# Squared-ReLU attention and two MLPs: the short last row of each batch read from mirror blocks, loads two tiles a time, MLP steps at row ends

## The chip, the core and the metric

The program runs on one core of a Trainium2 chip. TensorE (PE) multiplies, with a separate record for the loading of weights (PEld); VectorE (DVE) and ScalarE (ACT) work elementwise; GpSimd (POOL) and SyncE (SP) mostly issue DMAs here. The metric is the device time of one execution in microseconds, as the median of several.

## What is computed

```python
B, S, D = 2, 3008, 256          # d_qk = 64, d_ff = 2048
scores = z @ z.T / S            # per batch, symmetric
x = u * (relu(scores)**2 @ v)   # 6016 x 256 over both batches
h = x @ w_in                    # first MLP, w_in and w_out given as float64 ("moe")
P = a[0] + a[1]*h + a[2]*h**2 + a[3]*h**3
Q = 1 + abs(b[0])*abs(h) + abs(b[1])*h**2
x = (P / (Q + 1e-6)) @ w_out
h = x @ w_in2                   # second MLP ("moe2")
out = (max(h, 0) + alpha*min(h, 0)) @ w_out2
```

## The kernel before

All products are made from fp32 values split into a high and a low part, so one product takes several matmuls: high by high, high by low, low by high.

**Attention.** A batch has six query blocks j, here called rows: five of 512 queries and a last one of 448 (`qn`). Keys go in pairs of 128-key tiles, 12 pairs kp in a batch, and a *step* is one row with one pair: 12 steps a row, 144 in both batches. A key block kb = kp // 2 has the 512 keys (or last 448) of the query block with that number. A *direct* step in `a_scores` makes four score matmuls (two tiles, two matmuls each with zA and zB), then ScalarE takes ReLU and scale out of PSUM (L836, L844) and squares (L849), and `hi_lo` splits the result r into ahi (ScalarE, L438) and alo (VectorE, L443). Since scores are symmetric, a block above the diagonal is the transpose of one below. Where `folded(b, j, kb)` holds, the direct step is followed by `turn_block`: VectorE transposes r in 32 x 32 pieces into rt (L760), and four DMAs write it to DRAM (L771). When row kb later comes to that pair, its step is *folded*: no score matmuls, one load of rr from DRAM (L804), then `hi_lo`. Before, `folded` asks for a full 512-query row, so the last row of a batch is direct in all 12 steps. `in_turns` mixes folded and direct steps of a row evenly. Rows of 512 queries hold their columns in a permuted order (`q_side`, and `swap` on the host) that the piecewise transposes bring about; the last row does not.

Three steps later (`LAG_A`), `a_values` multiplies r with v: 8 matmuls for ahi (L870) and 4 for alo (L881), into one accumulator. At the end of a row, `a_end` loads u and multiplies on VectorE (L914), which frees the accumulator for the next row, and writes the product to DRAM for the MLP.

`load_z` and `load_v` load and split z and v: all of a batch's tiles are put into the program at the start of its first row. v is split by a cast (ScalarE, for the most part) and a subtraction (VectorE, L443) into vt.

**MLPs.** 6016 tokens go in 12 blocks, each with 8 steps in either MLP. A step has 12 matmuls into h or m (L941 to L943) and 12 back (L870, L881). A first-MLP step has seven VectorE operations on 128 x 1024 (L1000 to L1012) and six on ScalarE; a second-MLP step two and three. Weights are decoded from float64 (`weight`), those of the first MLP stay in SBUF, those of the second go to DRAM and come back in 16 fills (`fill_w`, L641) through GpSimd's queue, all put in at the end of attention.

**Order.** The program is put down in one order for TensorE; for the other engines and SP's queue a planner (`Plan.order`) sorts by due times, worked backward from TensorE's order. While the attention steps are put down, `plan.debt` adds VectorE's planned time and subtracts `FILL` times TensorE's; whenever it is below `DEBT` (plus `EDGE` where a row has just ended, which is seen at the third step of the next row), the next item of a list `extra` is put in: a weight or a first-MLP step (from step `HEAD` on). `X1` first-MLP steps are in the list; the rest runs in the tail with the second MLP, after attention. SBUF work tiles share 48 equal rooms.

Of the kernel before, what the change touches and what calls it, by code (L numbers as in the profile page):

```python
# [28 lines left out]

WIRE = 0.6  # L30

FILL, DEBT, EDGE = 0.95, 4.0, 4.0

LAG_A, LAG_M = 3, 2

HEAD, X1 = 40, 21

R0, RD = 2, 2.5

# [259 lines left out]
def relu2_attention_rational_mlp_prelu_mlp(  # L299
# [13 lines left out]
    nc = tc.nc  # L313
    P = 128
# [5 lines left out]
    NJ = NF // 2  # L320
    QB = 512
    NQ = -(-S // QB)
    NK = -(-S // P)
    NKP = NK // 2
# [4 lines left out]
    qn = [min(QB, S - j * QB) for j in range(NQ)]  # L329
# [10 lines left out]
    plan = Plan({"p": PT, "z": ZP, "x": XP, "s": 2, "h": 1, "acc0": 1, "acc1": 1, "m": 1, "sr": 1})  # L340
# [12 lines left out]
    def room(nm, dtype=F32, shape=(P, 2, QB)):  # L353
        return Buf("p", lambda i: pt.tile(list(shape), dtype, tag=f"p{i}", name=nm))

    def big_room(nm):
        return room(nm, F32R, (P, 2, 2, 256))
# [10 lines left out]
    def h_room(nm):  # L368
        return Buf("h", lambda i: at["h"][i])
# [15 lines left out]
    def in_dram(shape, nm, parts=1, dtype=F32):  # L385
        t = dr.tile(shape, dtype, name=nm)
        return Buf(None, lambda _: t, parts)
# [7 lines left out]
    def pe(cols, count, fn, r, w):  # L395
        return plan.add("PE", count * (cols / 2400 + 0.0136), fn, r, w)

    def sp(kb, fn, r, w, level="load", rate=210.0, horizon=NEAR):
        return plan.add("SP", 0.5, fn, r, w, level, after=3.0, data=kb / rate, horizon=horizon)

    def pool_dma(kb, fn, r, w, level="dec", rate=180.0, horizon=FAR):
        return plan.add("POOL", 1.1, fn, r, w, level, after=3.0, data=kb / rate, horizon=horizon)
# [233 lines left out]
    def fill_w(store, jp, in_room):  # L636
        d = store[jp]
        t = room("w", F32R, (P, 2, 2, 256)) if in_room else big_room("w")
        pool_dma(
            512,  # L640
            lambda: nc.gpsimd.dma_start(out=t().rearrange("p k c d -> p k (c d)"), in_=d()),  # L641
            [d],
            [t],
            level="load",
            rate=250.0,
        )
        store[jp] = t

    zA = {}

    zB = {}

    def q_side(z, b, j):

        if qn[j] < QB:
            return z[b, j]()[:, : qn[j]]
        return z[b, j]().rearrange("p (s a r) -> p a s r", s=4, a=4)

    def load_z(b, g):

# [71 lines left out]
        zB[b, j] = t  # L732

    def folded(b, i, j):
        return i < j and qn[j] == QB

    def in_turns(b, j):
        first = [kp for kp in range(NKP) if folded(b, kp // 2, j)]
# [7 lines left out]
    order = {q: in_turns(*q) for q in blocks}  # L746

    direct = [0]
    turned = {}

    def turn_block(b, j, kp, r):

        kb, h = kp // 2, kp % 2
        if (b, j, kb) not in turned:
            turned[b, j, kb] = in_dram([4, P, QB], f"rt{b}_{j}_{kb}", 8)
        d = turned[b, j, kb]
        t = room("rt", F32, (P, 4, 4, 2, 32))
        dve(
            1024,
            lambda: nc.vector.transpose(  # L760
                t().rearrange("p s a i x -> p i a s x"), r().rearrange("p i (g x) -> p i g x", x=32)
            ),
            [r],
            [t],
            level="turn",
        )
        for a in range(4):
            x0 = a * P + h * 64
            sp(
                128,  # L770
                lambda a=a, x0=x0: nc.sync.dma_start(  # L771
                    out=d()[:, :, x0 : x0 + 64].rearrange("s (a r) x -> r (s a) x", r=32),
                    in_=t()[32 * a : 32 * a + 32].rearrange("r s a i x -> r (s a) (i x)"),
                ),
                [t],
                [(d, 4 * h + a)],
                rate=150.0,
            )
# [18 lines left out]
    def a_scores(b, j, kp):  # L797
        n = qn[j]
        if folded(b, kp // 2, j):
            r, d = room("rr"), turned[b, kp // 2, j]  # L800
            s0 = kp % 2 * 2
            sp(
                512,
                lambda: nc.sync.dma_start(out=r(), in_=d()[s0 : s0 + 2].rearrange("s p k -> p s k")),  # L804
                [d],
                [r],
            )
            ahl[b, j, kp] = hi_lo(r, n, kp)
            return
        r = room("r")  # L810

        pair = None
        if not opened:
            turn = kp % 3 if (b, j) == (0, 0) else direct[0] % 2
            direct[0] += 1
            if turn == 1:
                pair = h_room("sp")
            elif turn == 2:
                t2 = Buf("acc1", lambda i: at["acc1"][i])
                pair = t2  # L820
        for i in range(2):
            k = 2 * kp + i
            zk = zA[b, k // 4]
            s = (pair, i) if pair is not None else s_room("s")
            ks = slice((k % 4) * P, (k % 4 + 1) * P)

            def mm(s=s, i=i, zk=zk, ks=ks):
                o = pair()[:, i, :n] if pair is not None else s()[:, :n]
                nc.tensor.matmul(o, zk()[:, ks], q_side(zA, b, j), start=True, stop=False)  # L829
                nc.tensor.matmul(o, zk()[:, ks], q_side(zB, b, j), start=False, stop=True)  # L830

            pe(n, 2, mm, [zk, zA[b, j], zB[b, j]], [s])
            if pair is None:
                act(
                    n,
                    lambda s=s, i=i: nc.scalar.activation(r()[:, i, :n], s()[:, :n], AF.Relu, scale=1.0 / S),  # L836
                    [s],
                    [(r, i)],
                    psum=True,
                )  # L840
        if pair is not None:
            act(
                2 * n,
                lambda: nc.scalar.activation(r()[:, :, :n], pair()[:, :, :n], AF.Relu, scale=1.0 / S),  # L844
                [pair],
                [r],
                psum=True,
            )
        act(2 * n, lambda: nc.scalar.activation(r()[:, :, :n], r()[:, :, :n], AF.Square), [r], [r])  # L849
        ahl[b, j, kp] = hi_lo(r, n, kp)  # L850
        if folded(b, j, kp // 2):
            turn_block(b, j, kp, r)
# [274 lines left out]
    edge, done = [], []  # L1127

    def a_stream():

        pend = []

        def drain(upto):
            while len(pend) > upto:
                q, kp = pend.pop(0)
                a_values(*q, kp)
                if kp == order[q][-1]:
                    a_end(*q)
                    edge.append(True)

        for g in range(NQ):
            load_z(0, g)
            if g % 2 == 0 and g < NQ:
                load_v(0, 2 * g)
                load_v(0, 2 * g + 2)
        for q in blocks:
            b, j = q
            if j == 0 and b:
                for g in range(NQ):
                    load_z(b, g)  # L1150
                for kp in range(0, NKP, 2):
                    load_v(b, kp)
            a_begin(*q)
            for kp in order[q]:
                a_scores(b, j, kp)
                pend.append((q, kp))
                drain(LAG_A)
                yield
        drain(0)
        yield  # L1160
# [23 lines left out]
    fills = list(w2)  # L1184

    extra = []
# [3 lines left out]
    for k in range(max(rest, 2 * NJ)):  # L1190
        extra += [("m",)] * ((k + 1) * rest // (2 * NJ) - k * rest // (2 * NJ))
        extra += [("w", w2.pop(0), False)]
    n1 = 0
    for st in range(NB * NKP + 1):
        edge.clear()
        next(ga)
        while extra and plan.debt < DEBT + (EDGE if edge else 0):
            if st < R0:
                break
            what = next((x for x in extra if x[0] == "w" or st >= HEAD), None)  # L1200
            if what is None:
                break
            if what[0] == "w" and st < HEAD and st - R0 < RD * (sum(x[0] == "w" for x in done)):
                break
            extra.remove(what)
            done.append(what)
            if what[0] == "w":
                weight(*what[1], what[2])
            else:
                opened.append(n1)  # L1210
                next(g1s)
                next(g1s)
                n1 += 1
                edge.clear()
    for what in extra:
        if what[0] == "w":
            weight(*what[1], what[2])
    for k, f in enumerate(fills):
        fill_w(f[1], f[2], False)

    left = (NB - 1) * NJ - KEEP
    steps = NB * NJ - n1
    for st in range(steps):
        more = (st + 1) * left // steps - st * left // steps
        next(g1s)
        if st:
            next(g2s)
        if more:
            next(g2s)
        next(g1s)  # L1230
        if more > 1:
            next(g2s)
            next(g2s)
# [54 lines left out]
```

## Time and profile before

| | |
|---|---|
| median of 3 runs | 1531.78 us (1531.62 to 1534.46) |
| the profiled execution | 1532.52 us |
| its span | 1530.3 us |
| TensorE busy | 1512.1 us, 6736 matmuls |
| VectorE busy | 1393.6 us |
| ScalarE busy | 1224.8 us |
| granted TensorE clock, mean | 0.999 |

Attention takes about the first 600 us; batch 1 starts a little after 300 us. The tail holds the MLPs up to the end. Matmul ends are modelled, so the distance from one start to the next is read rather than the duration of one. A wait is the idle time of an engine before an instruction, put down to what released it.

### The profile page before, as it was taken

What the parts mean: (1) busy time and instruction counts of PE and PEld (TensorE: products, weight loads), DVE (VectorE), ACT (ScalarE), POOL (GpSimd) and SP (SyncE); (2) the same over time, 40 slices, a digit from 0 to 9 for tenths busy, and PEclk for the clock granted to TensorE, in tenths of its full rate; (3) what the DMA queues carried; (4) which work ended last, traced back from release to release, by engine and by line L of the source; (5) the groups of instructions that cost most, each with busy time, mean ns of one, the idle gap of its engine ahead of it and who ended that gap; (6) DMA issues with size and microseconds to landing.
All of it is one profiled execution on the core that took longest, in us unless ns stands there. A gap on an engine that the chain in (4) does not pass through costs nothing.

```text
span 1530.3 us, 17886 instructions
## 1 busy us (share of the span) xinstructions
PE 1512.1 (99%) x6736; PEld 1261.2 (82%) x6736; DVE 1393.6 (91%) x1429; ACT 1224.8 (80%) x1465; POOL 73.2 (5%) x98
## 2 busy tenths in 40 slices
PE   9999999999999999999999999999999999999999
PEld 7887888867788888788888888888888888888888
DVE  8999898997999996899999999999999999999963
ACT  8888888996987988878778787777877777787754
POOL 1000010011112112000000000000000000000000
PEclk9999999999999999999999999999999999999999
DMA  6986431545765635300000000000000000000000
GB/s 188 227 229 182 123 102 68 182 105 147 204 178 169 225 125 170 130 28 28 28 28 14 28 29 14 28 14 28 29 28 28 28 14 28 28 25 28 15 1 24
DMA packets 131207, 126.14 MB, mean 82 GB/s; under 512 B 90145, under 2 KB 99889, under 8 KB 131121
## 3 DMA queue, kind: packets, MB, share of 16 engines
q1 hardware_dynamic: 121488, 90.40, 19.9%
q0 software_dynamic: 9632, 34.62, 6.9%
q8 instruction: 52, 0.85, 0.2%
q14 instruction: 35, 0.28, 0.1%
HBM read 74.72 MB, written 47.45 MB: 80 GB/s over the span
## 4 chain that ended last, share of the span: by engine, by line
PE 87%; DVE 7%; ACT 3%; issue 1%; DMA 1%; SPq 1%; DVEq 0%; ACTq 0%
PE acc L870 33%; PE acc L881 17%; PE h L943 5%; PE h L941 5%; PE h L942 5%; PE m L943 5%; PE m L941 5%; PE m L942 5%; PE s L830 1%; PE s L829 1%; DVE alo L443 1%; PE acc L860 1%; ACT r L836 1%; ACT r L849 1%; DVE vt L443 0%
## 5 line engine op out<-in xcount | busy, mean ns | idle before, releaser
L870 PE MATMUL acc<-ghi,w 128*128 128x512 f32 (+1 forms) x1472 | 360.7, 387 | 0.0
L870 PEld LDWEIGHTS acc<-ghi,w 128*128 128x128 f32 x1472 | 275.6, 188 | 54.9
L870 PE MATMUL acc<-ahi,vt 128*128 128x512 f32 (+1 forms) x1152 | 284.8, 389 | 5.8 <-DVE ut L914 4.9
L870 PEld LDWEIGHTS acc<-ahi,vt 128*128 128x128 f32 x1152 | 216.6, 188 | 51.4 <-DVE ut L914 4.8
L997 ACT ACTIVATE t<-h,sc 128x1024 f32<-128x1024 f32 (+1 forms) x96 | 114.1, 1188 | 107.5 <-PE h L943 103.9
L881 PE MATMUL acc<-glo,w 128*128 128x512 f32 (+1 forms) x736 | 195.3, 387 | 1.9 <-DVE glo L1012 1.9
L1064 ACT ACTIVATE m<-m,sc 128x512 f32<-128x512 f32 (+1 forms) x182 | 117.8, 692 | 67.9 <-PE m L943 67.7
L1000 DVE SCALAR_TENSOR_TENSOR ab<-sq,cb,ab 128x1024 f32<-128x1024 f32 (+1 forms) x96 | 121.2, 1262 | 50.5 <-ACT sq L995 49.9
L881 PEld LDWEIGHTS acc<-glo,w 128*128 128x128 f32 x736 | 137.7, 188 | 30.2 <-DVE glo L1012 2.8
L943 PE MATMUL h<-xhi,w 128*128 128x512 f32 (+1 forms) x404 | 154.6, 383 | 0.0
L942 PE MATMUL h<-xlo,w 128*128 128x512 f32 (+1 forms) x404 | 154.6, 383 | 0.0
L941 PE MATMUL h<-xhi,w 128*128 128x512 f32 (+1 forms) x404 | 154.6, 383 | 0.0
L881 PE MATMUL acc<-alo,vt 128*128 128x512 f32 (+1 forms) x552 | 147.4, 387 | 1.5 <-DVE alo L443 1.5
L943 PE MATMUL m<-xhi,w 128*128 128x512 f32 (+1 forms) x364 | 140.8, 387 | 0.0
L942 PE MATMUL m<-xlo,w 128*128 128x512 f32 (+1 forms) x364 | 140.8, 387 | 0.0
L941 PE MATMUL m<-xhi,w 128*128 128x512 f32 (+1 forms) x364 | 140.7, 387 | 0.0
L443 DVE TENSOR_TENSOR glo<-m,ghi 128x1024 fp32r<-128x1024 f32 (+1 forms) x96 | 115.1, 1199 | 11.8 <-ACT ghi L438 11.8
L1005 ACT ACTIVATE sq<-ab,one 128x1024 f32<-128x1024 f32 (+1 forms) x96 | 110.3, 1149 | 17.1 <-DVE t L1002 16.8
L881 PEld LDWEIGHTS acc<-alo,vt 128*128 128x128 f32 x552 | 103.9, 189 | 22.8 <-DVE alo L443 2.7
L1009 DVE TENSOR_TENSOR ghi<-t,sq 128x1024 fp32r<-128x1024 f32 (+1 forms) x96 | 115.5, 1203 | 7.8 <-ACT sq L1006 6.8
L836 ACT ACTIVATE r<-s 128x512 f32<-128x512 f32 (+1 forms) x170 | 94.8, 601 | 32.0 <-PE s L830 31.4
L443 DVE TENSOR_TENSOR alo<-r,ahi 128x1024 fp32r<-128x1024 f32 (+1 forms) x92 | 108.9, 1188 | 11.9 <-ACT ahi L438 11.6
(99 smaller groups left out, 2726.3 us busy)
## 6 DMA issues: line engine op xcount, KB each, us to landing
rt<-rt SPq DMA_DIRECT2D x160, 128.0 KB, 3.5
rr<-rt SPq DMA_DIRECT2D x40, 512.0 KB, 4.9
wraw<-in_moe_w_in_dram POOLq DMA_DIRECT2D x16, 512.0 KB, 5.2
wraw<-in_moe_w_out_dram POOLq DMA_DIRECT2D x16, 512.0 KB, 4.9
wd<-dec POOLq DMA_DIRECT2D x16, 512.0 KB, 3.1
w<-wd POOLq DMA_DIRECT2D x16, 512.0 KB, 9.9
x2d<-x SPq DMA_DIRECT2D x11, 512.0 KB, 2.6
xr<-x2d SPq DMA_DIRECT2D x11, 512.0 KB, 3.2
```

The source lines that it names most:

```text
L443: lambda: nc.vector.tensor_tensor(lo(), src(), hi().bitcast(F32), ALU.subtract),
L836: lambda s=s, i=i: nc.scalar.activation(r()[:, i, :n], s()[:, :n], AF.Relu, scale=1.0 / S),
L870: nc.tensor.matmul(acc()[:, e, :n], w()[:, k, i, e * P : (e + 1) * P], hi()[:, i, :n], start=first and i == 0 and k == 0, stop=False,)
L881: nc.tensor.matmul(acc()[:, e, :n], w()[:, 0, i, e * P : (e + 1) * P], lo()[:, i, :n], start=False, stop=last and i == both - 1,)
L941: nc.tensor.matmul(acc, w_hi, hi, start=first, stop=False)
L942: nc.tensor.matmul(acc, w_hi, lo, start=False, stop=False)
L943: nc.tensor.matmul(acc, w_lo, hi, start=False, stop=last)
L997: act(N, lambda: activation(c(t), c(h), AF.Identity, scale=a3, bias=a2), [h], [t], psum=True, ptr=2, **kw)
L1000: dve(N, lambda: stt(c(ab), c(sq), b1, c(ab), ALU.mult, ALU.add), [sq, ab], [ab], ptr=1, **kw)
L1005: act(N, lambda: activation(c(sq), c(ab), AF.Abs_reciprocal_sqrt, bias=one), [ab], [sq], ptr=1, **kw)
L1009: dve(N, lambda: tt(c(hi), c(t), c(sq), ALU.mult), [t, sq], [hi], **kw)
L1064: lambda i=i, f=f: nc.scalar.activation(t()[:, i, :n], h()[:, i, :n], AF.Copy, scale=al[:, f : f + 1]),
```

## The change

The last row's blocks are folded too. In rows 0 to 4, the direct steps of pairs 10 and 11 are now turned and written (448 or fewer columns, in pieces of 64 or 32 columns of fp32), and 10 of the last row's 12 steps load rr of 448 columns. For that the last row's columns are permuted as well, in two parts of 256 and 192, so its two direct steps take eight matmuls of those widths instead of four of 448.

The first six loads are put down ahead of batch 0, the rest one at each step of its first row; those of batch 1 two at every second step of batch 0's last row. At the end of a row a first-MLP step that is ready goes before a weight. `HEAD` goes from 40 to 38, `X1` from 21 to 18, `FILL` from 0.95 to 0.97. The fills of the second MLP's weights are put in as six at the end of attention and two for each second-MLP step.

```diff
-FILL, DEBT, EDGE = 0.95, 4.0, 4.0
+FIRST, NEXT = 6, 4
+FILL, DEBT, EDGE = 0.97, 4.0, 4.0
...
-HEAD, X1 = 40, 21
+HEAD, X1 = 38, 18
...
-        if qn[j] < QB:
-            return z[b, j]()[:, : qn[j]]
-        return z[b, j]().rearrange("p (s a r) -> p a s r", s=4, a=4)
+        t = z[b, j]().rearrange("p (s a r) -> p a s r", s=4, a=4)
+        if qn[j] == QB:
+            return [(0, QB, t)]
+        return [(0, QB // 2, t[:, 0:2]), (QB // 2, qn[j], t[:, 2:4, 0:3])]
...
     def folded(b, i, j):
-        return i < j and qn[j] == QB
+        return i < j
...
         if (b, j, kb) not in turned:
-            turned[b, j, kb] = in_dram([4, P, QB], f"rt{b}_{j}_{kb}", 8)
+            turned[b, j, kb] = in_dram([4, P, qn[kb]], f"rt{b}_{j}_{kb}", 8)
         d = turned[b, j, kb]
...
             x0 = a * P + h * 64
+            wide = 64
+            if qn[kb] < QB and a >= 2:
+                x0 = QB // 2 + (a - 2) * 96 + h * 64
+                wide -= 32 * h
             sp(
-                128,
-                lambda a=a, x0=x0: nc.sync.dma_start(
-                    out=d()[:, :, x0 : x0 + 64].rearrange("s (a r) x -> r (s a) x", r=32),
-                    in_=t()[32 * a : 32 * a + 32].rearrange("r s a i x -> r (s a) (i x)"),
+                2 * wide,
+                lambda a=a, x0=x0, wide=wide: nc.sync.dma_start(
+                    out=d()[:, :, x0 : x0 + wide].rearrange("s (a r) x -> r (s a) x", r=32),
+                    in_=t()[32 * a : 32 * a + 32].rearrange("r s a i x -> r (s a) (i x)")[:, :, 0:wide],
                 ),
...
             sp(
-                512,
-                lambda: nc.sync.dma_start(out=r(), in_=d()[s0 : s0 + 2].rearrange("s p k -> p s k")),
+                n,
+                lambda: nc.sync.dma_start(out=r()[:, :, :n], in_=d()[s0 : s0 + 2].rearrange("s p k -> p s k")),
                 [d],
...
                 o = pair()[:, i, :n] if pair is not None else s()[:, :n]
-                nc.tensor.matmul(o, zk()[:, ks], q_side(zA, b, j), start=True, stop=False)
-                nc.tensor.matmul(o, zk()[:, ks], q_side(zB, b, j), start=False, stop=True)
-            pe(n, 2, mm, [zk, zA[b, j], zB[b, j]], [s])
+                for (c0, c1, x), (_, _, y) in zip(q_side(zA, b, j), q_side(zB, b, j)):
+                    nc.tensor.matmul(o[:, c0:c1], zk()[:, ks], x, start=True, stop=False)
+                    nc.tensor.matmul(o[:, c0:c1], zk()[:, ks], y, start=False, stop=True)
+            pe(n, 2 if n == QB else 4, mm, [zk, zA[b, j], zB[b, j]], [s])
             if pair is None:
...
-        for g in range(NQ):
-            load_z(0, g)
-            if g % 2 == 0 and g < NQ:
-                load_v(0, 2 * g)
-                load_v(0, 2 * g + 2)
+        todo = [("z", 0, 0), ("v", 0, 0), ("z", 0, 1), ("v", 0, 2)]
+        todo += [x for g in range(2, NQ) for x in (("z", 0, g), ("v", 0, 2 * g))]
+        def load(count):
+            for _ in range(count):
+                if todo:
+                    kind, b, k = todo.pop(0)
+                    (load_z if kind == "z" else load_v)(b, k)
+        load(FIRST)
         for q in blocks:
             b, j = q
-            if j == 0 and b:
-                for g in range(NQ):
-                    load_z(b, g)
-                for kp in range(0, NKP, 2):
-                    load_v(b, kp)
+            if b and j == 0:
+                load(1)
             a_begin(*q)
-            for kp in order[q]:
+            for i, kp in enumerate(order[q]):
+                if q == (0, 0):
+                    load(1)
+                elif b == 0 and j == NQ - 1 and i == NEXT - 1:
+                    todo = [x for g in range(NQ) for x in (("z", 1, g), ("v", 1, 2 * g))]
+                if todo and q != (0, 0) and i % 2 == 1:
+                    load(2)
                 a_scores(b, j, kp)
...
     n1 = 0
+    nw = 0
     for st in range(NB * NKP + 1):
...
         next(ga)
-        while extra and plan.debt < DEBT + (EDGE if edge else 0):
-            if st < R0:
+        while extra and st >= R0 and plan.debt < DEBT + (EDGE if edge else 0):
+            ready = st >= HEAD and (n1 < min(nw // 2, NJ) or n1 >= NJ)
+            k = next((k for k, x in enumerate(extra) if (x[0] == "m" and ready) or (x[0] == "w" and not (edge and ready and ("m",) in extra))), None)
+            if k is None or (extra[k][0] == "w" and st < HEAD and st - R0 < RD * nw):
                 break
-            what = next((x for x in extra if x[0] == "w" or st >= HEAD), None)
-            if what is None:
-                break
-            if what[0] == "w" and st < HEAD and st - R0 < RD * (sum(x[0] == "w" for x in done)):
-                break
-            extra.remove(what)
-            done.append(what)
+            what = extra.pop(k)
             if what[0] == "w":
                 weight(*what[1], what[2])
+                nw += 1
             else:
...
             weight(*what[1], what[2])
-    for k, f in enumerate(fills):
-        fill_w(f[1], f[2], False)
+    fill = [lambda f=f: fill_w(f[1], f[2], False) for f in fills]
+    def top(count):
+        for _ in range(min(count, len(fill))):
+            fill.pop(0)()
+    top(6)
...
         more = (st + 1) * left // steps - st * left // steps
+        top(2 * more)
         next(g1s)
...
     swap[:whole] = swap[:whole].reshape(-1, 4, 4, 32).transpose(0, 2, 1, 3).reshape(-1)
+    ends = [whole + 128 * s + 32 * a for a in range(4) for s in range(4) if 128 * s + 32 * a < seq - whole]
+    swap[whole:] = (_np.array(ends)[:, None] + _np.arange(32)).reshape(-1)
     for name in _INS:
```

## Rows read from the trace of the kernel before

**Rows 1.** The page: busy us, share of the span, instructions of each engine.

```profile
PE 1512.1 (99%) x6736; PEld 1261.2 (82%) x6736; DVE 1393.6 (91%) x1429; ACT 1224.8 (80%) x1465; POOL 73.2 (5%) x98
```

**Rows 2.** Stretches: us, busy us (instructions) by engine, granted clock, DMA share, GB/s.

```profile
core 0: us, PE busy (x) PEld busy (x) DVE busy (x) ACT busy (x) POOL busy (x), PEclk, DMA share, GB/s
0.00:300.00 300.00, 294.84 (x1294) 244.70 (x1295) 273.56 (x340) 259.19 (x323) 20.15 (x32) 1.00 0.57 164
300.00:600.00 300.00, 292.66 (x1279) 240.25 (x1278) 275.79 (x325) 258.23 (x337) 45.59 (x52) 0.99 0.54 161
425.00:575.00 150.00, 150.00 (x662) 124.08 (x662) 147.15 (x175) 125.48 (x157) 26.84 (x29) 1.00 0.53 168
50.00:100.00 50.00, 50.00 (x219) 40.75 (x218) 47.47 (x68) 43.94 (x57) 3.62 (x5) 1.00 0.88 228
358.00:362.00 4.00, 4.00 (x11) 3.15 (x12) 2.17 (x3) 4.00 (x6) 1.11 (x2) 0.57 0.59 198
900.00:1100.00 200.00, 200.00 (x884) 165.62 (x883) 191.03 (x171) 157.09 (x176) 0.00 (x0) 1.00 0.07 24
```

**Rows 3.** Waits, TensorE: us in total, times, longest.

```profile
PE acc L870 <- DVE ut L914: 4.9, 4, 1.8
PE s L829 <- ACT r L836: 2.2, 4, 0.8
PE acc L881 <- DVE glo L1012: 1.9, 2, 1.7
PE acc L881 <- DVE alo L443: 1.5, 3, 0.7
PE acc L870 <- DVE vt L443: 0.9, 1, 0.9
```

**Rows 4.** Timeline, TensorE, 300 to 360: start, us, instructions, idle time before.

```profile
316.60 1.90 PE L870 MATMUL acc<-ahi,vt 128*128 128x512 f32 x7 [0.90 <-DVE vt L443]
...
357.92 3.38 PE L870 MATMUL acc<-ahi,vt 128*128 128x512 f32 x8 [1.80 <-DVE ut L914]
```

**Rows 5.** Timeline, TensorE, one step of batch 0's last row.

```profile
257.22 0.36 PE L829 MATMUL s<-zA 128*128 128x448 f32 x1
...
258.02 1.79 PE L870 MATMUL acc<-ahi,vt 128*128 128x448 f32 x8
...
260.46 0.36 PE L829 MATMUL s<-zA 128*128 128x448 f32 x1
```

**Rows 6.** Timeline, TensorE, the last 384 tokens.

```profile
1505.54 0.33 PE L941 MATMUL m<-xhi,w 128*128 128x384 f32 x1
1505.71 0.33 PE L942 MATMUL m<-xlo,w 128*128 128x384 f32 x1
```

**Rows 7.** Groups by shape: busy us, mean ns, idle us before; score weight loads.

```profile
L829 PEld LDWEIGHTS s<-zA 128*128 128x128 f32 x170 | 32.2, 190 | 11.1 <-ACT r L836 3.9 <-DVE zA L682 1.4
```

**Rows 8.** Timeline, VectorE, 327 to 331.

```profile
327.53 2.37 DVE L760 STREAM_TRANSPOSE rt<-r 128x1024 f32<-128x1024 f32 x2
329.81 1.19 DVE L443 TENSOR_TENSOR alo<-r,ahi 128x1024 fp32r<-128x1024 f32 x1
```

**Rows 9.** Groups by shape, VectorE, 0 to 610.

```profile
L760 DVE STREAM_TRANSPOSE rt<-r 128x1024 f32<-128x1024 f32 x40 | 49.0, 1236 | 4.1 <-DMA rt<-rt 4.1
...
L1000 DVE SCALAR_TENSOR_TENSOR ab<-sq,cb,ab 128x1024 f32<-128x1024 f32 x21 | 27.0, 1287 | 13.4 <-ACT sq L995 13.3
...
L1011 DVE TENSOR_TENSOR t<-t,ab 128x1024 f32<-128x1024 f32 x21 | 25.6, 1221 | 0.1
```

**Rows 10.** DMA issues: instructions, KB of one, median us to landing.

```profile
rt<-rt SPq DMA_DIRECT2D x160, 128.0 KB, 3.5
rr<-rt SPq DMA_DIRECT2D x40, 512.0 KB, 4.9
...
w<-wd POOLq DMA_DIRECT2D x16, 512.0 KB, 9.9
...
zB<-zA SPq DMA_DIRECT2D x18, 128.0 KB, 3.9
```

**Rows 11.** Waits of VectorE and ScalarE on transfers of blocks.

```profile
DVE rt L760 <- DMA rt<-rt: 4.1, 2, 2.5
...
ACT ahi L438 <- DMA rr<-rt: 3.2, 2, 2.1
```

## The prediction

> **What bounds the kernel now.** I read the page's busy times first, then who waits for whom on TensorE, then busy times by stretch, and last the timeline of the places that these point to. TensorE is busy for 1512.1 us of 1530.3, VectorE for 1393.6 [rows 1]. A busy TensorE need not be at its peak, so look at the spacing: in the steady MLP stretch 884 matmuls fill 200 us, 0.226 us each, and 512 columns at 2.4 GHz are 0.213 of that [rows 2]. TensorE is the bound, at its pace, and VectorE runs 95.5% beside it there. All named waits of TensorE on other engines that matter come to some 11 us [rows 3]: 4.9 at four ends of rows (the values of the next row need the accumulator that VectorE still has to multiply with u), 4.6 for score evictions, vt and alo, 1.9 for glo. One of the row ends also cost clock: after 1.80 us of idle time [rows 4] the granted clock stood at 0.57 over 358 to 362 us, the 1.2 GHz level for most of it, and 11 matmuls ran where 17.7 would have [rows 2]; 6.7 times 0.226 is 1.5 us. So two things can move the time: fewer matmuls, and fewer stalls. VectorE bounds nothing on average but has little left.
>
> **Scores no longer computed.** The last row of each batch now takes 10 of its 12 steps from mirror blocks, 20 in all. Such a step before has four 448-column score matmuls, from 257.22 to 258.02 us: 0.80 us [rows 5]. All of it is on TensorE's path, in line with the value matmuls behind it (the step takes 3.24 us, it will take 2.44). 20 x 0.80 = **16.0 us less**. ScalarE loses two evictions and a square each time, which bound nothing in that row and are worth nothing by themselves.
>
> **The remaining four direct steps** of those rows issue eight matmuls of 256 and 192 columns where four of 448 stood: the same columns, 16 more instructions. Low end: a 384-column matmul follows the next by 0.17 us [rows 6], 0.013 more than its columns at 2.4 GHz, so 16 x 0.013 = 0.2. High end: no matmul shorter than the 0.19 us of its weight load [rows 7]: 8 x 0.19 less 0.80 is 0.72 a step, 2.9 in all. The 384-column ones undercut 0.19 already, so I stay near the low end: **0.6 more**. The Trainium skill (TensorE: Matmul & The Clock Gate, LDWEIGHTS) puts a load of 128 columns at 107 ns and says that it overlaps the running matmul; an estimate by that page: only the 192-column ones (0.08 us) would be held up, 16 times some 0.015 us, and the term would be 0.4. No row here has a matmul that short at the full clock.
>
> **Work that the mirror costs.** The ten blocks a batch are now turned where they are computed, as their last two steps in rows 0 to 4: 20 transposes on VectorE, 1.19 us each in line (2.37 for two) [rows 8], 1.24 alone [rows 9], so 24 us; 80 more writes on SP's queue, each landing in 3.5 us, and 20 loads of rr, 4.9 us [rows 10]. Against that, three first-MLP steps leave the attention phase (21 to 18). Each has seven VectorE operations of 1.22 to 1.29 us, from 27.0 us for 21 to 25.6 us for 21 [rows 9], 8.7 us a step, 26 in all, and 24 x 0.226 = 5.4 us of TensorE, 16.3 in all. So VectorE's work in the attention phase stays as it was, 273.56 + 275.79 = 549 us of the first 600 [rows 2], now about 547, while TensorE's part shrinks: 600 less 15.4 (the two terms above) less 16.3 less the stalls below (9) is 559 us. That is a share of 97.9% instead of 91.6%. This is the weak point of the forecast. Look at 425 to 575 us: VectorE is busy 147.15 of 150 us, 98.1%, and TensorE has no idle time [rows 2]. Such a share can be carried for 150 us by this order of work. Low end 0; high end, if the phase gets only halfway from 91.6 to 98.1%, 547 / 0.949 = 576, 17 us late. I take **3 more**, since the 150 us row is the nearest to what the whole phase will look like.
>
> The three steps that moved make the tail richer in VectorE work: 78 first-MLP steps for the same number of second ones (two VectorE operations each, so 2.4 us against 5.4 on TensorE). Scaling the 95.5% of [rows 2] by that mix gives 96.6%. Under the 98.1% just shown, so 0. The tail's TensorE work is only moved, not added.
>
> **Queues.** SP gets 100 more issues in 560 us at about half a microsecond each; they sit behind each other, not behind compute. The rr loads of a row queue ahead of the next batch's z and v on SP; ScalarE's cast of rr and through it the row's values are what waits if one is late. Over 40 loads that was 3.2 us of ScalarE [rows 11], none of it seen on TensorE; 20 more at that rate would be 1.6. I take **0.5**, from 0 to 1.6. The DMA engines were busy for 88% of 50 to 100 us and TensorE was not idle there [rows 2].
>
> **Loads two tiles a time.** Batch 1's z and v are issued through the last row of batch 0 instead of all being due at the start of batch 1. Before, their splits meet that batch's first row; TensorE waits there for vt (0.90 us at 316.60 [rows 4]) and four times for evictions that queue behind vt casts on ScalarE, 2.2 us [rows 3]. With alo's share this is about 3.5 us; 3.0 of it goes, as the last row now has few evictions of its own. What is late next there is the row end itself. The head of the kernel waits for the first z all the same: 0.
>
> **MLP steps at row ends.** The first one is now allowed from step 38, which is where the end of row 2 falls, and at an end an MLP step goes before a weight. 5.4 us of matmuls cover the 1.8 us of the longest such wait. Of 4.9 us and the 1.5 of lost clock I take 4.5 back. But the cover of one end gets thinner: between the last values of row 4 and the first of row 5 a direct score step (0.80 us) stood, and now none does, as the fourth step of that row is a mirrored one. Should no MLP step land there, both batches pay 1.8 + 1.5, so 0 to 6.6; I take **1.0**, since the rule asks for one.
>
> **Weight fills.** 16 fills of w were issued together at the end of attention and landed in 9.9 us [rows 10]; now six, then two per second-MLP step. VectorE's wait-free start of the tail should give back 1.5 of the 1.9 us that TensorE waited for glo [rows 3]. The cover for the later fills is three MLP steps of over 10 us; without it, one landing, 9.9 us. Stalls given back: 3.0 + 4.5 + 1.5 = **9.0 less**.
>
> **Sum.** 1530.3 - 16.0 + 0.6 + 3.0 + 0.5 + 1.0 - 9.0 = 1510.4 us of span. The profiled execution took 1532.5, 2.2 more than its span, and is 0.7 above the median of the runs, 1531.8. So 1510.4 + 2.2 - 0.7 = **1512 us**, 1.3% faster. A measurement of this kernel can tell about 0.2%, 3.1 us, from no change.
>
> **Rivals.** First, only the matmuls go and the stalls stay, moved to other places, because every stall is VectorE or ScalarE being late and both of these get denser: 1512 + 9 = 1521. For it: VectorE's share rises. Against it: ScalarE, which released 2.2 us of them, gets less to do. Chance 0.22.
>
> Second, slower than before: VectorE becomes the bound of the attention phase. Place: steps 0 to 144. If no batch can sustain more than the 91.6% that it shows now, the 547 us take 597 instead of 559, 38 us where I took 3, and the time is 1547: the phase is as long as it was and the tail has 16.3 us more. It decides at 93.7%: then the phase takes 600 - 16.3 us and nothing is gained. For it: neither of the two 300 us rows is above 92%. Against it: in both, the idle time of VectorE sits at the head and around the batch border, and 425 to 575 us is at 98.1% [rows 2]. Chance 0.07.
>
> Third, the transfers bind in rows 0 and 1, where eight of the 20 added blocks are written. VectorE has waited twice for a transpose buffer still being written, 4.1 us in all [rows 11]; were each of the eight to cost 2.05, it is 16 us, and with the fuller VectorE nothing would make up for it: 1528. Against it: 88% DMA share passed without harm. Chance 0.05. A rule speaks for it: the Trainium skill (DMA: Bandwidth & Descriptors, Specifications) wants at least 512 B a piece, below which a read-modify-write sets in; these writes are in pieces of 256 and 128 B. In the trace a 128 KB rt write of such pieces lands in 3.5 us and the 128 KB zB copy in 3.9 [rows 10], so the penalty does not show at the landing time.
>
> Last, the code might mirror fewer steps than it says (0.01, no change), or the stalls vanish altogether and VectorE costs nothing, under 1504 (0.05).
>
> **How the numbers follow.** Forecast, 1504 to 1517: 0.60. Faster by over 0.2%: forecast 0.60, better 0.05, first rival 0.22, and 0.03 of the third: 0.90. Within 0.2%: 0.02 of the third, 0.02 of the second, 0.01: 0.05. Slower: 0.05 of the second. Range: down to 1504 (terms of 3.0, 1.0, 0.5 and 0.4 at their low ends and the last 3 us of stalls gone), up to 1524, which takes in the first rival and most of VectorE's high end; the rest is left out.
>
> **What would show it.** 60 rr loads, 60 transposes, 84 x 4 score matmuls' worth of columns; a folded step of the last row taking 2.44 us; VectorE near 98% over the attention phase with TensorE idle under 5 us there; no wait for ut over 1 us after row 2; none for vt at the batch border. Wrong would be: attention's VectorE share under 94% with TensorE waiting for alo or glo all over (second rival), waits for rr or rt buffers in rows 0, 1 and 5 (third), or waits of the old size at the ends of rows and the border (first).

## The result

The changed kernel takes 1513.5 us (median; 1511.4 to 1514.6) against 1532.6 of the kernel before, run beside it: a ratio of 0.9872, 95% interval 0.9855 to 0.9889. 1512 was forecast. The total was right. How it comes about was not: the next sections show that the two halves of the sum, 16 us from matmuls and 9 us from stalls, cannot be had one without the other.

The busy times on the page of the changed kernel, as in [rows 1]:

```profile
PE 1497.1 (99%) x6672; PEld 1248.8 (83%) x6672; DVE 1410.0 (93%) x1449; ACT 1193.2 (79%) x1406; POOL 79.2 (5%) x98
```

Its stretches, with the columns of [rows 2]: attention up to the last values matmul at 569.4 us, the start of the tail, and the steady MLP stretch.

```profile
0.00:569.40 569.40, 560.93 (x2473) 464.01 (x2474) 541.46 (x658) 469.30 (x585) 72.27 (x86) 1.00 0.72 203
569.40:620.00 50.60, 46.89 (x194) 37.87 (x193) 46.17 (x46) 37.81 (x43) 5.88 (x12) 0.93 0.44 145
900.00:1100.00 200.00, 200.00 (x884) 165.64 (x883) 192.05 (x173) 158.69 (x176) 0.00 (x0) 1.00 0.06 22
```

Attention and the start of the tail in the kernel before, where the last values matmul ends at 607.7 us:

```profile
0.00:607.70 607.70, 595.20 (x2609) 491.93 (x2610) 553.90 (x671) 521.12 (x665) 70.53 (x93) 1.00 0.55 162
607.70:660.00 52.30, 50.37 (x221) 40.99 (x220) 42.01 (x38) 40.37 (x45) 2.67 (x5) 1.00 0.39 139
```

Attention became 38.3 us shorter (607.7 to 569.4), the tail 20.8 longer (1530.3 - 607.7 = 922.6 to 1512.8 - 569.4 = 943.4): 17.5 us off the span. By its own terms the prediction had 34.7 off attention and 14.8 more in the tail. So attention did 3.6 better than its terms and the tail 6.0 worse, and the two partly cancel. Most of the tail's 6.0 lies at its start: 194 matmuls in 50.6 us at a mean clock of 0.93, where before 221 ran in 52.3 at the full one. At 0.226 us each, 6.7 us are lost there against 2.3 before. The steady tail is untouched: 884 matmuls in 200 us, with VectorE at 96.0% (96.6 was forecast).

TensorE's waits in the changed kernel, as in [rows 3], those of its first 15 us left out:

```profile
PE acc L878 <- DVE ahi L796: 3.3, 2, 2.1
PE acc L889 <- DVE glo L1020: 3.2, 1, 3.2
PE m L949 <- DVE m L1078: 0.5, 1, 0.5
PE acc L878 <- ACT ahi L792: 0.4, 1, 0.4
PE acc L878 <- DVE ut L922: 0.4, 1, 0.4
```

And the two largest in TensorE's timeline of the same kernel:

```profile
548.88 1.86 PE L878 MATMUL acc<-ahi,vt 128*128 128x448 f32 x4 [2.13 <-DVE ahi L796]
...
596.99 2.08 PE L889 MATMUL acc<-glo,w 128*128 128x512 f32 x4 [3.17 <-DVE glo L1020]
598.87 0.63 PE L949 MATMUL h<-xhi,w 128*128 128x512 f32 x1
599.29 0.63 PE L950 MATMUL h<-xlo,w 128*128 128x512 f32 x1
```

The waits for u at row ends are gone but for 0.4 us (4.9 before), and so are those at the batch border, about 3.5 us. In their place stand a wait in each batch's last row (1.2 and 2.1 us), for the half-tile correction that VectorE makes for pair 11 (L796), and a longer one for glo where the tail starts. After the 3.17 us of idle time matmuls start 0.42 us apart instead of 0.226: the lower clock level, a granted clock of 0.50 from 597 to 603 us.

### The profile page after: what moved, and what is told of

Read it like the earlier page. It is cut to its first block, busy times and chain, and to the rows that moved or that the text cites. A ratio compares the mean times of both kernels' runs of the same rounds, so it can differ in the third digit from the quotient of the medians.

```text
span 1512.8 us, 17898 instructions
## 1 busy us (share of the span) xinstructions
PE 1497.1 (99%) x6672; PEld 1248.8 (83%) x6672; DVE 1410.0 (93%) x1449; ACT 1193.2 (79%) x1406; POOL 79.2 (5%) x98
## 4 chain that ended last, share of the span: by engine, by line
PE 74%; DVE 8%; issue 2%; ACT 1%; DMA 0%; SPq 0%; DVEq 0%; ACTq 0%
PE acc L878 26%; PE acc L889 13%; PE m L949 5%; PE m L950 5%; PE m L951 5%; PE h L949 5%; PE h L950 5%; PE h L951 5%; DVE alo L445 2%; PE acc L868 1%; PE s L837 1%; PE s L838 1%; DVE t L1019 1%; DVE ab L1018 1%; DMA rt<-rt 0%
## 5 line engine op out<-in xcount | busy, mean ns | idle before, releaser
L1078 DVE TENSOR_TENSOR m<-m 128x1024 f32<-128x1024 f32 (+1 forms) x91 | 109.7, 1205 | 11.6 <-ACT m L1072 11.5
L1020 DVE TENSOR_TENSOR glo<-t,sq 128x1024 fp32r<-128x1024 f32 (+1 forms) x96 | 114.7, 1195 | 1.4
```

Source lines behind the costliest of these rows:

```text
L1020: dve(N, lambda: tt(c(lo), c(t), c(sq), ALU.mult), [t, sq], [lo], **kw)
```

## The experiments

Each kernel ran beside the kernel before; ratios are to that, so 0.9872 is what the whole change gives. "The arrangement" is everything in the change but the mirrored last row: loads, row-end rule, `HEAD`, `X1`, `FILL` and fills.

### The mirrored row alone, and the rest alone

`fold_only`, the kernel before with the hunks of `q_side`, `folded`, `turn_block`, `a_scores` and `swap`:

```diff
-        return i < j and qn[j] == QB
+        return i < j
```

> The kernel before with the mirrored last row alone: 64 fewer matmuls, but loads, the rule at row ends, the list of MLP steps (21, from step 40, fill 0.95) and the weight fills as they were. Theory (TensorE is the bound and the matmuls are the gain; the other parts give and take stalls): 1532.6 less the 15.8 us of matmuls, stalls as before or some us more, 1515 to 1522. Rival (VectorE sets the attention phase, and only the shift of three MLP steps into the tail pays for the 24 us of transposes): 1530 or more.

Measured: 1534.9 us, ratio 1.0019 (1.0009 to 1.0028). The matmuls went and the time stayed. The rival's number was right. Its stretches, attention up to 581.2 us and what follows:

```profile
0.00:581.20 581.20, 565.19 (x2473) 466.83 (x2474) 531.26 (x634) 468.04 (x579) 69.73 (x79) 0.99 0.69 194
581.20:640.00 58.80, 46.84 (x191) 36.60 (x190) 57.53 (x71) 40.32 (x48) 15.16 (x20) 0.94 0.56 188
```

And TensorE's longest waits in it:

```profile
PE acc L876 <- DVE ut L920: 8.9, 5, 2.7
PE acc L887 <- DVE glo L1018: 6.3, 2, 4.8
PE acc L887 <- DVE alo L443: 3.3, 2, 2.6
```

Look at 581 to 640 us: VectorE is busy for 57.53 of 58.80 us while TensorE is idle for 12. Work for VectorE that belongs to the attention phase has been left for the start of the tail; the last weight's decoding (its addition, L575) starts at 608.8 us there, 27.6 us after attention's end, where before it started at 598.4, ahead of the end. That is not all of it: for the same 2473 matmuls attention is 11.8 us longer than in the changed kernel (581.2 against 569.4), the rest 8.4 (951.8 against 943.4), so more than half of the 20 us between the two is lost inside attention.

`no_fold`, the changed kernel with those same hunks undone:

```diff
-        return i < j
+        return i < j and qn[j] == QB
```

> The changed kernel without the mirrored last row: loads, row ends, step list and fills are the new ones. Theory: the full number of matmuls, the waits for u at row ends and at the batch border gone (some 10 us of lost time before), a new wait of some 6 us where the tail starts: 1526 to 1530. Rival (the gain is mostly the freed stalls): 1518 or less.

Measured: 1530.7 us, ratio 0.9985 (0.9976 to 0.9994). The arrangement alone gives 0.15%, some 2 us, just above the range expected here and far from the 9 us of the prediction. Its waits on TensorE (a part of them): those for u are gone but for 0.6 us, and others have come.

```profile
PE acc L883 <- DVE glo L1014: 2.8, 1, 2.8
PE s L831 <- ACT r L838: 2.1, 3, 0.9
PE h L945 <- DVE w L445: 1.5, 1, 1.5
PE acc L872 <- DVE ut L916: 0.6, 1, 0.6
```

So one half costs 0.2%, the other gives 0.15%, and both together give 1.28%. On the new arrangement the mirrored row is worth 0.9985 - 0.9872 = 1.1%, 17 us, the 16 of its matmuls and a little; on the old one it is worth less than nothing. I read this as the arrangement making room for the 24 us of transposes; the next runs test it.

### How much room VectorE has

`turn_twice`, the changed kernel with each of the 20 added blocks transposed twice:

```diff
+        def turn():
+            for _ in range(2 if qn[kb] < QB else 1):
+                nc.vector.transpose(...)
```

> The changed kernel with each of the 20 added blocks transposed twice on VectorE, everything else in the same order: 20 x 1.19 = 24 us more VectorE work in the attention phase, which there is at 541 us of 569. Theory (VectorE has little left, 95% busy): some of it shows, 4 to 15 us. Rival 1 (VectorE is already the bound of the phase): 20 us or more. Rival 2 (it has slack that the transposes fill): under 3 us.

Measured: 1533.5 us, ratio 1.0008 (0.9998 to 1.0017), 1.36% or 21 us above the changed kernel. The number is that of rival 1. Its attention phase, ending at 590.5 us:

```profile
0.00:590.50 590.50, 569.35 (x2473) 465.52 (x2474) 566.55 (x680) 471.56 (x586) 70.81 (x88) 0.99 0.70 196
```

The same 2473 matmuls, 25.1 us more of VectorE (541.46 to 566.55), and the phase is 21.1 us longer, 0.84 us for each. But the cost is not spread evenly. Both kernels issue the same matmuls in the same order, so stretches between the same matmuls can be laid side by side. Four of the changed kernel:

```profile
135.00:235.00 100.00, 100.00 (x444) 82.50 (x443) 96.35 (x104) 82.67 (x97) 2.89 (x4) 1.00 0.56 156
235.00:262.00 27.00, 25.80 (x127) 22.92 (x126) 26.81 (x31) 21.23 (x26) 0.00 (x0) 1.00 0.74 240
460.00:500.00 40.00, 40.00 (x178) 32.95 (x176) 39.90 (x49) 32.40 (x39) 7.01 (x8) 1.00 0.81 232
500.00:550.00 50.00, 47.44 (x222) 40.55 (x221) 49.88 (x69) 37.17 (x48) 12.75 (x13) 0.98 0.78 251
```

And the same four in `turn_twice`:

```profile
135.40:236.50 101.10, 100.25 (x444) 82.39 (x443) 99.44 (x106) 79.23 (x92) 3.04 (x4) 1.00 0.53 152
236.50:270.20 33.70, 28.54 (x129) 23.99 (x129) 33.51 (x38) 25.59 (x33) 0.00 (x0) 0.96 0.73 222
474.40:514.60 40.20, 40.20 (x177) 32.62 (x175) 40.04 (x50) 30.73 (x36) 5.84 (x8) 1.00 0.79 221
514.60:571.10 56.50, 49.55 (x226) 41.62 (x226) 56.30 (x75) 41.11 (x53) 11.23 (x14) 0.97 0.73 232
```

Before the first of them, 523 matmuls take 120.0 us in both kernels, with five of the added blocks in the stretch. All ten of batch 0 start before 236.5 us and have cost about 1.5 us by then; 6.7 more come out in the next stretch, 27 us in the changed kernel, where VectorE was full already (26.81 us) and now has 38 operations to do instead of 31. In batch 1, 6.2 are lost from 345 to 460 us, where VectorE was at 96.8%, and 6.5 from 500 to 550, where it was at 99.8%. Between them, a stretch at 99.6% loses 0.2. So VectorE bounds parts of the phase, the ends of the batches above all, and lets work in for nothing elsewhere; the mean shares of 95.1 and 95.9% are no ceiling. With 8.5 us of 569 idle on TensorE, the page calls the whole phase bound by TensorE.

`x1_21`, `x1_16`: the changed kernel with 21 or 16 MLP steps in the list instead of 18.

```diff
-HEAD, X1 = 38, 18
+HEAD, X1 = 38, 21    # the other: 38, 16
```

> The whole changed kernel with 21 MLP steps in the list instead of 18: everything else, loads, row ends and fills, is the new form. Two weights are then left over at the end of attention. Theory A: slower by the VectorE time of three MLP steps less what their 16.3 us of TensorE work gives in the phase, 5 to 12 us, 1519 to 1526, with longer waits where the tail starts. Theory B: within 2 us of 1513.5.

> The whole changed kernel with 16 MLP steps in the list: the last weight is put in at step 138 of 144 instead of 143. Theory A: VectorE gets through before the tail, the 3.2 us wait for glo at the tail's start with its stretch at the lower clock and the waits of the last row shrink: 1508 to 1512; the tail then has 80 first-MLP steps and must not wait for VectorE. Rival: VectorE's share in the tail, 96.6% by the sum, goes to some 97.4% and shows there: 1514 or more.

Measured: with 21 steps 1523.1 us, ratio 0.9938 (0.9923 to 0.9953), 0.66% or 10 us slower than with 18. With 16 steps 1515.5 us, ratio 0.9887 (0.9873 to 0.9902), whose interval overlaps that of 18: no gain. The wait for glo at the tail's start did not shrink with 16 either (3.2 us again), although the last weight's addition (L577) starts 2.7 us behind the end of attention there and 9.6 us behind it in the changed kernel. So the late last weight is not what makes it, and my reading of that wait was wrong. The wait stands some 27 us behind the end of attention in both kernels, and the kernel before has one of 1.69 us at the like place, 25.5 us behind. Its cause stays open. Attention and the start of the tail with 21:

```profile
0.00:578.40 578.40, 570.64 (x2521) 472.35 (x2522) 549.95 (x656) 479.63 (x593) 80.20 (x82) 1.00 0.70 196
578.40:640.00 61.60, 49.05 (x195) 37.99 (x195) 57.67 (x67) 41.84 (x50) 8.43 (x15) 0.94 0.47 153
```

The phase again holds VectorE at 95.1%, but that is no limit of VectorE either: the planner lets in what `FILL`, 0.97, allows, and two weights are left over. They, and one of the three further steps, come out as 12.6 us of idle TensorE at the start of the tail. With `FILL` at 0.95 the phase holds 93.3% (523.04 of 560.8 us in `fill95`, below).

### Which part of the arrangement

`fold_x18` adds to `fold_only` the shorter list alone; `fold_x18_loads` adds the new order of loads to that; `loads_old` and `fill95` undo one thing each in the changed kernel, as do `edge_old` and `fill_once`.

```diff
-HEAD, X1 = 40, 21
+HEAD, X1 = 40, 18    # fold_x18
```

> The kernel before with the mirrored last row and with 18 MLP steps in the list instead of 21; nothing else of the change. The list is not quite through at the end of attention (two weights are left over; with 21 steps three weights and two MLP steps were). Theory A (what ate the 16 us in the run with the mirrored row alone is VectorE work that does not fit into the shorter attention phase, and falls on the start of the tail): about half of the gain comes back, 1520 to 1527. Theory B (the loads, the row-end rule and the fills are what the mirrored row needs): no better than with 21 steps, 1532 or more.

Measured: 1533.2 us, ratio 1.0002 (0.9993 to 1.0012). Theory A in this form falls: fewer MLP steps alone bring nothing back. There is room and it is not used, as the stretch of its attention phase shows (with `FILL` at 0.95 two weights were left over): VectorE is at 521.74 of 574.3 us, 90.8%, and TensorE is idle for 18.5.

```profile
0.00:574.30 574.30, 555.82 (x2425) 458.40 (x2426) 521.74 (x627) 454.89 (x566) 67.08 (x78) 0.99 0.71 197
```

```diff
-        load(FIRST)
+        for g in range(NQ):
+            load_z(0, g)
+            ...                # loads_old: all at a batch's first row
```

> The changed kernel with the old order of loads: all z and v of a batch put in at the start of its first row. Row-end rule, 18 steps, fill 0.97 and weight fills are new. Theory C (with the last row mirrored, the old loads fall on the batch border together and block VectorE and ScalarE there; this is most of what the runs with the mirrored row on the old order lack): 1520 to 1527, with waits for u, alo and evictions between 240 and 330 us. Theory D (what they lack is the fill of 0.97, which lets the list of weights and MLP steps get through before attention ends): within 3 us of 1513.5.

Measured: 1522.9 us, ratio 0.9942 (0.9927 to 0.9957), 0.70% or 11 us slower than the whole change. Theory C. The stretch at its batch border:

```profile
277.00:306.00 29.00, 21.07 (x93) 16.78 (x91) 28.81 (x42) 28.29 (x42) 2.89 (x4) 0.95 0.17 56
```

The end of that stretch in VectorE's timeline:

```profile
300.82 3.70 DVE L445 TENSOR_TENSOR vt<-vraw,vt 128x512 fp32r<-128x512 f32 x6
304.44 2.75 DVE L445 TENSOR_TENSOR alo<-r,ahi 128x1024 fp32r<-128x1024 f32 x2
```

And in TensorE's:

```profile
305.91 2.08 PE L889 MATMUL acc<-alo,vt 128*128 128x512 f32 x4 [5.47 <-DVE alo L445]
```

VectorE is busy for 28.81 of 29 us, six splits of v stand ahead of one alo, and TensorE waits 5.47 us for that alo. Before the change the same clump cost 0.9 us for vt and a few short waits [rows 3, 4]; that the last row then kept TensorE on score matmuls for longer is my explanation, and no run tests it.

```diff
-FILL, DEBT, EDGE = 0.97, 4.0, 4.0
+FILL, DEBT, EDGE = 0.95, 4.0, 4.0    # fill95
```

> The changed kernel with VectorE's planned share of the attention phase at 0.95 as before instead of 0.97. Two weights are then left over when attention ends and are decoded at the start of the tail. Theory D: 1520 to 1527, and the lost time stands where the tail starts, as waits for glo and for evictions of h. Theory C: within 3 us of 1513.5.

Measured: 1520.4 us, ratio 0.9923 (0.9908 to 0.9937), 0.51% or 8 us slower. Theory D too. The loss lies in part where it should: the stretch after the end of attention at 560.8 us has 6.0 us of idle TensorE and a clock of 0.94, and at 0.226 us a matmul 10.2 us are lost there against 6.7 in the changed kernel. That is 3.5 of the 5.1 us between the two profiled executions.

```profile
560.80:620.00 59.20, 53.17 (x217) 42.40 (x216) 56.02 (x65) 46.20 (x53) 11.10 (x18) 0.94 0.46 152
```

```diff
+        load(FIRST)            # fold_x18_loads: the loads as in the change
-HEAD, X1 = 40, 21
+HEAD, X1 = 40, 18
```

> The kernel before with the mirrored last row, 18 MLP steps and the new order of loads; fill 0.95, row ends and weight fills are old. Theory C: the border is clean and most of the gain is there, 1514 to 1521. Theory D: the leftover weights still cost, 1526 to 1533. If both parts are needed, it lies between, 1520 to 1527.

Measured: 1524.9 us, ratio 0.9954 (0.9939 to 0.9969): between, as written for the case that both are needed. The loads are worth 0.48% here (1.0002 to 0.9954), and 0.70% in the changed kernel. From 0.9954 to 0.9872 are 0.82%; the fill of 0.97 accounts for 0.51 when it is taken out alone. The rest is not settled, since the other two parts, the row-end rule with `HEAD` back at 40 (`edge_old`) and the fills (`fill_once`), show nothing when they are taken out alone:

```diff
+            what = next((x for x in extra if x[0] == "w" or st >= HEAD), None)    # edge_old
+    for k, f in enumerate(fills):                                                # fill_once
+        fill_w(f[1], f[2], False)
```

> The changed kernel with the old rule for what is put in at the end of a row, and MLP steps from step 40; the list still has 18, fill 0.97, loads and weight fills new. The rule decides whether an MLP step covers the multiplication with u. Expected: the waits for u at row ends come back at some ends, 2 to 6 us, 1515 to 1520. If the row-end rule is worth nothing: within 1.5 us.

> The changed kernel with all 16 weight fills put in at the end of attention, as before the change. After the change TensorE waits 3.2 us for glo at the start of the tail and then runs at the lower clock level; before it waited 1.9 for it. If spreading the fills is the cause of the longer wait: 4 to 6 us faster than the changed kernel, 1508 or so. If the cause is VectorE work left over from attention (the last weight is put in at the very last step): the same within 2 us, or slower by the old gap in VectorE's work.

Measured: without the row-end rule and with `HEAD` at 40, 1513.6 us, ratio 0.9875 (0.9861 to 0.9890); with all fills at once 1513.5, ratio 0.9876 (0.9861 to 0.9891). Neither can be told from the changed kernel. In `edge_old` the waits for u did come back, as expected, and the time did not follow. Two of TensorE's waits in `edge_old`:

```profile
PE acc L878 <- DVE ut L922: 5.4, 4, 2.0
PE acc L889 <- DVE glo L1020: 2.1, 1, 2.1
```

That is 5.0 us more for u and 1.1 less for glo; its wait for ahi (L796) is 0.6 us instead of 3.3, and over the 50.6 us after the end of attention the clock is 0.97 instead of 0.93. With VectorE this full, the waits stood elsewhere and the time was the same.

### The transfers

`write_twice`, the changed kernel with each of the 80 added block writes issued twice:

```diff
+            def put(a=a, x0=x0, wide=wide):
+                for _ in range(2 if qn[kb] < QB else 1):
+                    nc.sync.dma_start(...)
```

> The changed kernel with each of the 80 added writes of mirror blocks issued twice on SP's queue, same source and place. This doubles the transfers that the change added in pieces of 256 and 128 B. If the DMA engines or the issue queue bind in rows 0 and 1, as the third rival of the prediction had it: 5 to 20 us slower. If they have room: within 2 us of 1513.5.

Measured: 1660.2 us, ratio 1.084 (1.081 to 1.087), far outside both expectations, and not for the reason in either. The wait of SP's queue for those transfers (us, times, longest):

```profile
SPq L778 <- DMA rt<-rt: 199.8, 80, 6.4
```

A second write to the same place waits for the first one to land, on SP's queue, 2.5 us each, and everything behind it waits too. The rr loads come late: ScalarE waits 108.1 us for them, where it waited 9.8 in the changed kernel, and TensorE stands idle behind it. The DMA engines were at 61% from 100 to 300 us in this run, no fuller than in the changed kernel (63%). So it measured a blocked queue, not the room of the DMA engines. On that, only the changed kernel itself speaks. Its transposes, in the groups by shape (columns as in [rows 9]), never waited for a buffer, where before they had for 4.1 us [rows 11], with a DMA share of 0.72 over the attention phase instead of 0.55.

```profile
L763 DVE STREAM_TRANSPOSE rt<-r 128x1024 f32<-128x1024 f32 x60 | 74.1, 1236 | 0.0
```

## Why the prediction was right, and where its reasons were not

**Matmuls, 16.0 less.** Right as work: a folded step of the last row takes 2.44 us (559.52 to 561.96), as worked out, and 64 matmuls are gone. Wrong as a term that stands by itself: `fold_only` shows the same matmuls gone and nothing gained. Two such steps in TensorE's timeline of the changed kernel:

```profile
559.52 1.78 PE L878 MATMUL acc<-ahi,vt 128*128 128x448 f32 x8
561.14 0.97 PE L889 MATMUL acc<-alo,vt 128*128 128x448 f32 x4
561.96 1.38 PE L878 MATMUL acc<-ahi,vt 128*128 128x448 f32 x6
```

**Eight small matmuls, 0.6.** They take 0.89 us a step where four took 0.80, so 0.36 us in all, in the same timeline:

```profile
536.87 0.28 PE L837 MATMUL s<-zA 128*128 128x256 f32 x1
536.99 0.28 PE L838 MATMUL s<-zB,zA 128*128 128x256 f32 x1
537.10 0.25 PE L837 MATMUL s<-zA 128*128 128x192 f32 x1
537.19 0.28 PE L838 MATMUL s<-zB,zA 128*128 128x192 f32 x1
...
537.76 1.60 PE L878 MATMUL acc<-ahi,vt 128*128 128x448 f32 x7
```

The estimate by the Trainium skill (TensorE: Matmul & The Clock Gate, LDWEIGHTS), 0.4, was nearer than mine. The 192-column matmuls start 0.09 to 0.11 us before the next, so no load of 0.19 us held them up.

**VectorE, 3 more, from 0 to 17.** This is the step whose reason failed. It took the 98.1% of one 150 us stretch for what a whole phase can carry, and looked for 97.9% with TensorE idle under 5 us. The phase came out at 95.1% and 8.5 us. Single stretches carried 98 to 99.8%, so a share is not what limits it; `turn_twice` shows that the limit is local. The term is not measured by itself. Its sum, 26 us of MLP steps out against 24 us of transposes in, was right as a count, and `x1_21` shows what it is worth: with the three steps back in the list, 10 us. Two things in it were off. The phase was taken as 600 us, and its last values matmul ends at 607.7. And not all of VectorE's work stayed in it: up to the end of attention VectorE did 541.5 us, 12.4 less than before and not 2. A part of the last weight's decoding and the last four operations of the 18th step, some 9 us, ran behind the end, at the start of the tail. There VectorE was busy for 46.17 of 50.6 us, 91%, where before it was 42.01 of 52.3, 80%. The prediction had looked at the steady tail alone. The second rival had the mechanism in part. With the old arrangement the mirrored row holds VectorE at 91.4% (531.26 of 581.2 us in `fold_only`), the 91.6% of the rival, and ends at 1534.9, on the rival's side; but that share is no limit of VectorE, since the same row gets to 92.7% with fewer steps and the new loads (`fold_x18_loads`, 524.53 of 565.6 us) and to 95.1% with a `FILL` of 0.97 and the rest.

**Stalls, 9.0 less.** Wrong as a term: `no_fold` puts it at 2 us. The part for row ends (4.5) and that for fills (1.5) are zero within the measurement, some 2 us each way; the part for loads (3.0) is 7 to 11 us with the last row mirrored; without it no run tests the loads alone, and the whole arrangement gives 2. In the changed kernel the row ends and the border did clear; the start of the tail, where 1.5 was to come back, lost 4.4 more instead (6.7 against 2.3).

**The thin cover of the end of row 4, 1.0.** In the changed kernel no wait showed there. In `fold_only`, without the row-end rule, one did in batch 0, 2.14 us, near the 1.8 that the prediction named. The rule does not decide it: `fill95` has the rule and waits 2.11 us at the same place, and `edge_old` has not and does not wait there. `fold_only`, TensorE's timeline:

```profile
240.88 1.86 PE L876 MATMUL acc<-ahi,vt 128*128 128x448 f32 x8 [2.14 <-DVE ut L920]
```

**Queues, 0.5.** ScalarE waited for rr six times, 9.8 us, twice the rate that I took. The longest, 5.3 us, falls in the last row of batch 1. TensorE waited 0.4 us for a cast of ScalarE's (ahi L792) some 12 us later; whether that comes of it, no run tells. The term was good enough by luck of the cover more than by its working. The third rival, full DMA engines, did not show, and nor did the small pieces: a 128 KB write landed in 3.1 us in the median, one of the 64 KB writes that the change brings in 3.3.

The first rival (1521, stalls stay) turned out to be the price of a missing part of the arrangement: `fill95`, `loads_old` and `x1_21` sit at 1520 to 1523. That the total came out at 1513.5 is in part luck: 9 us of stalls were not to be had by themselves, the matmuls only with what was to remove them, and attention's 3.6 us too many met the tail's 6.0 too few.

## What to carry to other kernels

A busy engine at 99% with another at 91 to 93% beside it can be bound by both: add a known amount of work to the second and see what it costs, and in which stretches, before work is moved onto it (here 25 us cost 21, nearly all of it where VectorE stood at 97% or more already). A trade that moves work between engines and the schedule that makes room for it must be priced as one; taken apart, each half here was worth nothing. And where the engine that releases a wait has no time to spare, a wait that goes away need not be a gain: look for where it went.

## What the runs showed that I had not expected

Work added to VectorE did not cost TensorE anything where it was put, but later. The ten doubled transposes of batch 0 had cost about 1.5 us by 236.5 us, and 6.7 more came out in the 27 us behind them, with no block added there. The mean shares of the phase, 95.1 and 95.9%, show nothing of it. And 80 writes to places just written held SP's queue for 199.8 us and made the kernel 147 us slower (1660.2 against 1513.5), the dearest thing tried here.
